# Pinning the small work of an attention + squared-ReLU kernel to fixed places between the tile products

## The chip, the cores and the metric

One core of a Trainium2 chip runs the whole program. The metric is device time in microseconds (us). The engines named below are TensorE (PE, with its weight loads PEld), VectorE (DVE), ScalarE (ACT), GpSimd (POOL) and SyncE (SP), which here only issues transfers. Each engine works through its own list of instructions in order; semaphores make one wait for another.

## The reference

For each of 4 batches (12,480 rows of 128 numbers, 49 agents) agents attend to keys and values, queries attend to agents, and the product goes through a wide layer with a squared ReLU:

```python
def sm(a, b):
    s = scale * (a @ b.transpose(0, 2, 1))
    e = np.exp(s - s.max(-1, keepdims=True))
    return e / (e.sum(-1, keepdims=True) + 1e-09)
agent_v = sm(agents, k) @ v              # 49 x 128 per batch
x = sm(q, agents) @ agent_v              # 49,920 x 128 in all
h = np.maximum(x @ w_in, 0.0)            # 128 -> 2048
out = (h * h) @ w_out                    # 2048 -> 128
```

## The kernel before

The rows are cut into 52 groups of 960 (13 in each batch), a group into two halves of 480 columns. Because `sm(q, agents) @ agent_v @ w_in` is one small table times the query weights, the hidden layer is made from a per-batch table (`aw_hi`, `aw_ex`, 2048 columns, made by `tables`) and per-group query weights (`w`, `x`, made by `queries`). Numbers that must be exact are split into a rounded half and a rest (`hi`, `lo`; `g_hi`, `g_lo`), which TensorE multiplies one after the other.

The unit of the main loop is a *session*: two steps k and k+1, 416 sessions in all, 8 to a group and 104 to a batch. In a session TensorE does four products `h<-w,aw_hi` and four narrow ones `h<-x,aw_ex` (19 rows each, side by side) in `first`, and twelve products `o<-...` of the steps four back in `second`. For each of the two steps (`hidden`) ScalarE makes the ReLU `r<-h` and the square `g_hi<-r`, VectorE multiplies `r*h`, and the rest `g_lo` comes from GpSimd (step k, whose product stands in the tile `gg`: two instructions of 480) or from VectorE (step k+1, whose product `h<-r,h` stays in PSUM). The hidden tiles `h` are three pairs of PSUM banks, and a session uses two of them. So the second pair of products of a session is written over the tile of step k of the session before, and has to wait until VectorE has made `gg` from it.

Beside that runs small work for what comes next. For the next batch, `background`: 13 times `scores` (keys), `maxima`, 13 times `values`, `tables`. A value block is `d<-s,mb` on GpSimd, the exponential of `d` on ScalarE, a rounding cast on ScalarE and a difference on GpSimd for the weights `e` and for the values `vs`, and eight products into the one spare PSUM bank `psa`. For the next group, `queries`: eight products, a maximum and a subtraction on VectorE, an exponential on ScalarE, a sum, an addition and a reciprocal (`z`) on VectorE, a scaling on GpSimd (`e<-e,z`), cast and difference (`pp`), eight products with the identity `identr` that turn the weights over (L312, four to a half), a copy `w<-psa` on ScalarE, and five small copies by transfer for each half.

What sets the order: the main loop's own instructions on PE, ACT and DVE are chained in the order written (`queued`, L337). All small work, GpSimd's rests (L372) and all transfers are placed by the scheduler, which estimates when each becomes ready; `step` only spreads them over the sessions (`SPREAD`). The first batch's table and the first query weights are made ahead of the loop, whose first products start 83.71 us into the span.

Of the kernel before, what the change touches and what calls it, by code (L numbers as in the profile page):

```python
# [17 lines left out]
P = 128  # L18
# [10 lines left out]
QAT = 3  # L29
WIN = 4  # L30
# [4 lines left out]
SPREAD = 0.88  # L35
# [3 lines left out]
def agent_attention_relu2(ctx: ExitStack, tc: tile.TileContext, qT, kT, v, agT, w_in, w_out, outT):  # L39
    nc = tc.nc  # L40
    C, NTOK = qT.shape
# [9 lines left out]
    NQ = P // 32  # L51
    scale = 1.0 / math.sqrt(C)

# [6 lines left out]
    dec = ctx.enter_context(tc.tile_pool(name="dec", bufs=2))  # L60
    ps_h = ctx.enter_context(tc.tile_pool(name="ps_h", bufs=3, space=PSUM))
# [9 lines left out]
    identr = const.tile([TP, TP], F32R, name="identr")  # L71
    nc.scalar.copy(identr, ident[:TP, :TP])
# [54 lines left out]

    alone = [True]

    def bank():  # L130
        if alone[0]:
            return ps_h.tile([P, 2, 512], F32, name="h")[:, 0, :]
        return ps_a.tile([P, 512], F32, name="psa")


# [3 lines left out]
    def load_keys(b, i, pool, name):  # L139
        kt = pool.tile([C, BLK], F32, name=name)  # L140
        nc.sync.dma_start(kt, kT[:, b * N + i * BLK : b * N + (i + 1) * BLK])
        return kt

    def load_values(b, i, pool, name):
        vt = pool.tile([TP, NT, C], F32, name=name)
        src = v[b, i * BLK : (i + 1) * BLK, :].rearrange("(p t) c -> p t c", p=TP)
        last[nc.sync] = nc.sync.dma_start(vt, src)
        return vt

    def scores(b, i, kt):  # L150
        st = state.setdefault(b, {"s": []})
        ps = bank()
        sv = ps[:TP, : NT * NA].rearrange("p (t a) -> p t a", a=NA)
        for t in range(NT):
            nc.tensor.matmul(sv[:, t, :], kt[:, t * TP : (t + 1) * TP], ag[:, b, :], start=True, stop=True)  # L155
        yield
        s = sp.tile([TP, NT, NA], F32, name="s")
        nc.scalar.copy(s, sv)
        if i == 0:
            st["mx"] = small.tile([TP, NT, NA], F32, name="mx")  # L160
            nc.vector.tensor_copy(st["mx"], sv)
        else:
            nc.vector.tensor_max(st["mx"], st["mx"], sv)  # L163
        st["s"].append(s)

    def maxima(b):
        st = state[b]
        m1 = small.tile([TP, NA], F32, name="m1")
        nc.vector.reduce_max(m1, st["mx"].rearrange("p t a -> p a t"), axis=AX.X)
        yield  # L170
        pt = bank()
        nc.tensor.transpose(pt[:NA, :TP], m1, ident[:TP, :TP])
        yield
        m2 = small.tile([NA, 1], F32, name="m2")
        nc.vector.reduce_max(m2, pt[:NA, :TP], axis=AX.X)
        dg = small.tile([NA, NA], F32, name="dg")
        nc.vector.tensor_scalar_mul(dg, ident[:NA, :NA], m2)
        yield
        pb = bank()
        nc.tensor.matmul(pb[:TP, :NA], ones[:NA, :TP], dg, start=True, stop=True)  # L180
        yield
        st["mb"] = small.tile([TP, NA], F32, name="mb")
        nc.vector.tensor_copy(st["mb"], pb[:TP, :NA])

    def halves(out, x, n, eng):

        w = x.shape[2]
        nc.scalar.copy(out[:, :, :w], x)  # L188
        yield
        last[eng] = eng.tensor_sub(out[:, :, n : n + w], x, out[:, :, :w].bitcast(F32))  # L190

    def whole_values(b, i, vt):
# [10 lines left out]
        if i == 1:  # L203
            st["es"] = small.tile([TP, NT, NA], F32, name="es")
# [14 lines left out]
    def values(b, i, vt, eng):  # L219
        st = state[b]  # L220
        s = st["s"][i]
        mb = st["mb"].rearrange("p (o a) -> p o a", o=1).broadcast_to([TP, NT, NA])
        d = small.tile([TP, NT, NA], F32, name="d", bufs=2)
        eng.tensor_sub(d, s, mb)
        W = 2 * (C + 1)
        vs = split[i % 2]
        yield from halves(vs, vt, C + 1, nc.gpsimd)
        yield
        nc.scalar.activation(d, d, AF.Exp, scale=scale)
        e = small.tile([TP, NT, K2], F32R, name="e2", bufs=2)  # L230
        yield from halves(e, d, NA, eng)
        yield
        pv = bank()
        for t in range(NT):
            nc.tensor.matmul(pv[:K2, :W], e[:, t, :], vs[:, t, :], start=(t == 0), stop=(t == NT - 1))  # L235
        yield
        if i == 0:
            st["av"] = small.tile([K2, W], F32, name="av")
            nc.vector.tensor_copy(st["av"], pv[:K2, :W])
        else:  # L240
            nc.vector.tensor_add(st["av"], st["av"], pv[:K2, :W])  # L241

    def tables(b):
        st = state[b]
        qd = quad.rearrange("p h a -> p (h a)")
        if "x" not in st:
            st["x"] = small.tile([K2, C + 1], F32, name="x")
            nc.vector.tensor_add(st["x"], st["av"][:, : C + 1], st["av"][:, C + 1 :])
        x = st["x"]
        yield  # L250
        pa = bank()
        nc.tensor.matmul(pa[:C, :K2], x[:, :C], qd, start=True, stop=True)
        nc.tensor.matmul(pa[:K2, K2 : K2 + 1], qd, x[:, C:], start=True, stop=True)
        yield
        av = small.tile([C, K2], F32, name="avT")
        nc.scalar.copy(av, pa[:C, :K2])
        rl = small.tile([K2, 1], F32, name="rl")
        nc.vector.tensor_scalar_add(rl, pa[:K2, K2 : K2 + 1], 1e-9)
        nc.vector.reciprocal(rl, rl)
        hi = st["hi"] = aw.tile([P, FF], F32R, name="aw_hi")  # L260
        ex = st["lo"] = aw.tile([P, NCH // NQ, P], F32R, name="aw_ex")
        for n in range(FF // 512):
            yield
            cs = slice(n * 512, (n + 1) * 512)
            pw = bank()
            nc.tensor.matmul(pw[:K2, :], av, win[:, cs], start=True, stop=True)  # L266
            yield
            last[nc.scalar] = nc.scalar.activation(hi[:K2, cs], pw[:K2, :], AF.Copy, scale=rl)
            lo = aw.tile([NA, 512], F32R, name="aw_lo", bufs=3)
            last[nc.vector] = nc.vector.scalar_tensor_tensor(  # L270
# [3 lines left out]
            yield  # L274
            nc.sync.dma_start(hi[K2:, cs].bitcast(F32), lo[:SP, :].bitcast(F32))
            for t in range(NQ):
                nc.sync.dma_start(ex[t * 32 : t * 32 + NL, n, :].bitcast(F32), lo[SP:, t * P : (t + 1) * P].bitcast(F32))


    weights = {}  # L280

    def queries(g):
        b = g // NB
        qt = qp.tile([C, BLK], F32, name="qt", bufs=1)
        nc.sync.dma_start(qt, qT[:, g * BLK : (g + 1) * BLK])
        yield
        ps = bank()
        sv = ps[:TP, : NT * NA].rearrange("p (t a) -> p t a", a=NA)
        for t in range(NT):
            nc.tensor.matmul(sv[:, t, :], qt[:, t * TP : (t + 1) * TP], ag[:, b, :], start=True, stop=True)  # L290
        yield
        m = qp.tile([TP, NT, 1], F32, name="m", bufs=1)
        nc.vector.reduce_max(m, sv, axis=AX.X)
        e = qp.tile([TP, NT, NA], F32, name="e", bufs=1)
        nc.vector.tensor_sub(e, sv, m.broadcast_to([TP, NT, NA]))
        yield
        nc.scalar.activation(e, e, AF.Exp, scale=scale)
        yield
        z = qp.tile([TP, NT, 1], F32, name="z", bufs=1)
        nc.vector.reduce_sum(z, e, axis=AX.X)  # L300
        nc.vector.tensor_scalar_add(z, z, 1e-9)  # L301
        nc.vector.reciprocal(z, z)
        nc.gpsimd.tensor_mul(e, e, z.broadcast_to([TP, NT, NA]))
        yield
        pp = qp.tile([TP, NT, K2], F32R, name="pp", bufs=1)
        yield from halves(pp, e, NA, nc.gpsimd)
        weights[g] = []
        for j in range(2):
            yield
            pt = bank()  # L310
            for t in range(NT // 2):
                nc.tensor.matmul(  # L312
                    pt[:K2, t * TP : (t + 1) * TP], pp[:, j * (NT // 2) + t, :], identr, start=True, stop=True
                )
# [223 lines left out]
```

## Time and profile before

| | |
|---|---|
| three runs | 2061.34, 2061.95 (median), 2062.36 us |
| profiled execution | 2060.99 us, span 2059.2 us |
| granted TensorE clock, mean | 0.992 |
| busy: PE, ACT, DVE, POOL | 2029.8, 1782.3, 1686.1, 1279.2 us |
| largest POOL group, `g_lo` (L372) | 832 x 1222 ns |
| turning products `psa<-identr,pp` (L312) in the loop | 408 x 243 ns, in 102 places |

Busy time counts an engine as busy while any of its instructions runs. Matmuls overlap, so the time that a TensorE product really takes is read from the starts in the chain of waits or the timeline, not from its length. In the timeline a row has the start, the length, engine, line, operation, tiles written and read, shapes, count, and in brackets the idle time ahead and what ended it. `SPq` is SP's transfer queue, and the length there is what it took to issue the transfer.

### The profile page before, as it was taken

Reading aid. Unit: us, or ns where it says so; the run is one execution under the profiler, and the core shown is the slowest. Engines: PE = TensorE matmul, PEld = TensorE weight load, DVE = VectorE, ACT = ScalarE, POOL = GpSimd, SP = SyncE. Lnnn points to the kernel's source line nnn. Section 1 sums busy time; section 2 is a strip of 40 time slices with the busy share of each in tenths; the row PEclk is TensorE's granted clock in tenths of the full one; section 3 lists DMA queues with packets and bytes.
Section 4 is the critical chain, followed back from the end, with each engine's and each line's share of the span. In section 5 each row is a group of like instructions: output and inputs, shape, how many; then the busy total and the mean of one; then the engine's idle time right before and its main releaser. Section 6 shows DMA issues by size and latency. Waiting matters only on the chain.

```text
span 2059.2 us, 31857 instructions
## 1 busy us (share of the span) xinstructions
PE 2029.8 (99%) x11014; PEld 1589.8 (77%) x11014; DVE 1686.1 (82%) x1842; ACT 1782.3 (87%) x2100; POOL 1279.2 (62%) x1104
## 2 busy tenths in 40 slices
PE   9799999999999999999999999999999999999999
PEld 8588777777788777777778877777777777777777
DVE  5687888888887888888887788888888888888887
ACT  3478999989888899989888899998889898989897
POOL 3555787765544587776555467877555555656555
PEclk9799999999999999999999999999999999999999
DMA  9532122121122221221112212211111111111100
GB/s 288 160 92 76 59 72 74 53 77 41 45 81 65 62 72 54 72 71 57 55 54 69 68 42 61 74 58 49 42 50 36 45 36 46 37 41 36 38 23 20
DMA packets 55604, 131.36 MB, mean 64 GB/s; under 512 B 6660, under 2 KB 34388, under 8 KB 55444
## 3 DMA queue, kind: packets, MB, share of 16 engines
q1 hardware_dynamic: 55444, 129.33, 21.0%
q8 instruction: 88, 1.44, 0.3%
q14 instruction: 72, 0.59, 0.1%
HBM read 80.97 MB, written 25.56 MB: 52 GB/s over the span
## 4 chain that ended last, share of the span: by engine, by line
PE 53%; DVE 1%; issue 0%; ACT 0%
PE o L337 33%; PE h L337 16%; PE psa L290 2%; PE psa L155 1%; PE psa L312 1%; PE psa L235 1%; PE psa L266 0%; DVE h L337 0%; DVE gg L337 0%; DVE g_lo L337 0%; DVE z L301 0%; ACT r L337 0%; DVE ob L337 0%; ACT g_hi L337 0%; DVE av L241 0%
## 5 line engine op out<-in xcount | busy, mean ns | idle before, releaser
L372 POOL TENSOR_TENSOR g_lo<-gg,g_hi 128x480 fp32r<-128x480 f32 x832 | 999.2, 1222 | 685.7 <-DVE gg L337 489.1
L337 ACT ACTIVATE r<-h 128x960 f32<-128x960 f32 x832 | 800.9, 963 | 150.0 <-PE h L337 141.9
L337 ACT ACTIVATE g_hi<-r 128x960 fp32r<-128x960 f32 x832 | 837.7, 1007 | 34.1 <-POOL e L190 0.7
L337 DVE TENSOR_TENSOR h<-r,h 128x960 f32<-128x960 f32 x416 | 482.4, 1160 | 160.2 <-ACT r L337 157.8
L337 DVE TENSOR_TENSOR gg<-r,h 128x960 f32<-128x960 f32 x416 | 477.8, 1149 | 81.9 <-ACT r L337 81.0
L337 PE MATMUL o<-g_hi,wo_hi 128*128 128x480 f32 x1664 | 543.0, 408 | 0.0
L337 DVE TENSOR_TENSOR g_lo<-h,g_hi 128x960 fp32r<-128x960 f32 x416 | 480.8, 1156 | 45.2 <-ACT g_hi L337 8.1
L337 PE MATMUL o<-g_hi,wo_lo 128*128 128x480 f32 x1664 | 498.7, 381 | 0.0
L337 PE MATMUL o<-g_lo,wo_hi 128*128 128x480 f32 x1664 | 497.7, 380 | 0.0
L337 PE MATMUL h<-w,aw_hi 128*128 128x480 f32 x1664 | 483.3, 398 | 9.7 <-DVE gg L337 8.1
L337 PEld LDWEIGHTS o<-g_hi,wo_hi 128*128 128x128 f32 x1664 | 280.8, 188 | 118.8 <-issue 70.1
L337 PEld LDWEIGHTS o<-g_hi,wo_lo 128*128 128x128 f32 x1664 | 313.4, 188 | 51.3
L337 PEld LDWEIGHTS o<-g_lo,wo_hi 128*128 128x128 f32 x1664 | 313.0, 188 | 50.9
L337 PEld LDWEIGHTS h<-w,aw_hi 128*128 128x128 f32 x1664 | 289.0, 190 | 56.9 <-DVE gg L337 17.5
L337 PE MATMUL h<-x,aw_ex 19*128 19x480 f32 x1664 | 205.4, 481 | 0.1
L337 PEld LDWEIGHTS h<-x,aw_ex 19*128 19x128 f32 x1664 | 80.5, 182 | 140.7 <-issue 139.7
L290 PEld LDWEIGHTS psa<-ag,qt 128*120 128x120 f32 x816 | 102.2, 187 | 7.8 <-issue 1.4
L337 DVE COPY ob<-o 128x480 f32<-128x480 f32 x104 | 68.3, 656 | 39.8 <-PE o L337 38.3
L290 PE MATMUL psa<-ag,qt 128*120 128x49 f32 x816 | 98.1, 264 | 0.0
L190 POOL TENSOR_TENSOR vs<-vt,vs 120x1024 fp32r<-120x1024 f32 x39 | 86.3, 2213 | 16.7 <-ACT vs L188 16.4
L155 PEld LDWEIGHTS psa<-ag,kt 128*120 128x120 f32 x624 | 74.7, 185 | 4.8 <-DVE mx L163 0.6
L155 PE MATMUL psa<-ag,kt 128*120 128x49 f32 x624 | 71.9, 262 | 0.2 <-DVE mx L163 0.2
(109 smaller groups left out, 1026.6 us busy)
## 6 DMA issues: line engine op xcount, KB each, us to landing
qt<-in_qT SPq DMA_DIRECT2D x52, 480.0 KB
out_T<-ob SPq DMA_DIRECT2D x104, 240.0 KB
kt<-in_kT SPq DMA_DIRECT2D x39, 480.0 KB
vt<-in_v SPq DMA_DIRECT2D x39, 480.0 KB
x<-w SPq DMA_DIRECT2D x416, 35.6 KB
ahead<-in_kT SPq DMA_DIRECT2D x13, 480.0 KB
ahead<-in_v SPq DMA_DIRECT2D x13, 480.0 KB
w<-w SPq DMA_DIRECT2D x104, 56.2 KB
```

Source lines behind the costliest of these rows:

```text
L155: nc.tensor.matmul(sv[:, t, :], kt[:, t * TP : (t + 1) * TP], ag[:, b, :], start=True, stop=True)
L190: last[eng] = eng.tensor_sub(out[:, :, n : n + w], x, out[:, :, :w].bitcast(F32))
L235: nc.tensor.matmul(pv[:K2, :W], e[:, t, :], vs[:, t, :], start=(t == 0), stop=(t == NT - 1))
L290: nc.tensor.matmul(sv[:, t, :], qt[:, t * TP : (t + 1) * TP], ag[:, b, :], start=True, stop=True)
L312: nc.tensor.matmul(pt[:K2, t * TP : (t + 1) * TP], pp[:, j * (NT // 2) + t, :], identr, start=True, stop=True)
L337: ins = issue(*args, **kw)
L372: nc.gpsimd.tensor_sub(lo[:, n, :], gg[:, n, :], hi[:, n, :].bitcast(F32))
```

## The change

- Every instruction of the loop, small work, GpSimd's rests and SP's transfers included, is chained in the order written (`Pinned`). The scheduler no longer chooses.
- The small work is written as lanes of generators that ask for a place: "B" is a use of the spare bank, between the four main products (`main`) and the four narrow ones (`rest`); "A" and "D" are one piece for ScalarE and VectorE, behind step k's own work and again at the session's end; "G" and "S" are GpSimd's and SP's, at the session's end only. A session has room for one B, two G (a "GG" takes both) and three S.
- GpSimd takes over the roundings of the values, of their weights and of the query weights, which ScalarE did.
- The query weights are no longer turned by products and copied by ScalarE. VectorE turns 32x32 blocks (`et`), GpSimd rounds and takes the rest, two transfers write both to DRAM, eight transfers read them back in the new layout, and five copies fill the rest of `w` and `x` for both halves at once. Queries are 128 instead of 120 to a tile (the host pads them), and a group's chain starts nine sessions ahead.
- In `fill` each lane may move on by one piece; the query lane is asked first.

TensorE, ahead of a half's first session, before: the turning products stand among the main products.

```order
L337 MATMUL o<-g_lo,wo_hi 128x480 x2
L337 MATMUL h<-w_11444,aw_hi 128x480 x2
L312 MATMUL psa<-identr,pp 98x120 x4
L337 MATMUL h<-w_11444,aw_hi 128x480 x2
L337 MATMUL h<-x_11445,aw_ex 128x480 x4
L337 MATMUL o<-g_hi,wo_hi 128x480 x2
```

After, a session with a small piece on TensorE (`qt` are the queries, `ag` the agents):

```order
L64 MATMUL o<-g_lo,wo_hi 128x480 x2
L64 MATMUL h<-w,aw_hi 128x480 x4
L64 MATMUL psa<-ag,qt 128x49 x8
L64 MATMUL h<-x,aw_ex 128x480 x4
L64 MATMUL o<-g_hi,wo_hi 128x480 x2
```

The turning products are gone, and a small piece stands always between the main and the narrow products.

GpSimd at a value block before: `d` is taken ahead of the session's rests `g_lo`.

```order
L372 TENSOR_TENSOR g_lo_2535<-gg_2531,g_hi_2533 128x480 x2
L224 TENSOR_TENSOR d_3357<-s_1325,mb_1979 120x392
L190 TENSOR_TENSOR pp_2619<-e_2562,pp_2619 120x8x49
L372 TENSOR_TENSOR g_lo_2582<-gg_2578,g_hi_2580 128x480 x2
L372 TENSOR_TENSOR g_lo_2637<-gg_2633,g_hi_2635 128x480 x2
```

ScalarE before, at the same block: the exponential stands behind the squares of the session whose rest on GpSimd is `g_lo_2582`.

```order
L337 ACTIVATE g_hi_2580<-r_2576 128x960
L337 ACTIVATE r_2598<-h_2567 128x960
L337 ACTIVATE g_hi_2601<-r_2598 128x960
L229 ACTIVATE d_3357<-d_3357 120x392
L337 ACTIVATE r_2631<-h_2621 128x960
```

GpSimd at a value block after:

```order
L64 CAST vs1_107<-vt_2317 120x8x128
L64 TENSOR_TENSOR g_lo_2679<-gg_2675,g_hi_2677 128x480 x2
L64 TENSOR_TENSOR d_2707<-s_1137,mb_1849 120x392
L64 TENSOR_TENSOR g_lo_2726<-gg_2722,g_hi_2724 128x480 x2
L64 CAST e2_2751<-d_2707 120x8x49
```

ScalarE at that block after:

```order
L64 ACTIVATE g_hi_2677<-r_2673 128x960
L64 ACTIVATE r_2695<-h_2655 128x960
L64 ACTIVATE g_hi_2698<-r_2695 128x960
L64 ACTIVATE d_2707<-d_2707 120x392
L64 ACTIVATE r_2720<-h_2710 128x960
```

`d` now comes behind the session's rests, and its exponential still stands behind that same session's squares and ahead of the next session's first ReLU.

VectorE after, from a query's session on (`m` maximum, `z` sum and reciprocal, `et` the turned weights):

```order
L64 TENSOR_REDUCE m_2824<-psa_2802 128x8
L64 TENSOR_TENSOR qe_96<-psa_2802,m_2824 128x8x49
L64 TENSOR_TENSOR h_2797<-r_2841,h_2797 128x2x480
L64 TENSOR_TENSOR g_lo_2846<-h_2797,g_hi_2844 128x960
L64 TENSOR_REDUCE z_2850<-qe_96 128x8
L64 TENSOR_SCALAR z_2850<-z_2850 128x8
L64 RECIPROCAL z_2850<-z_2850 128x8
L64 TENSOR_TENSOR gg_2875<-r_2873,h_2854 128x960
L64 TENSOR_TENSOR av_2148<-av_2148,psa_2860 98x258
L64 TENSOR_TENSOR h_2855<-r_2895,h_2855 128x2x480
L64 TENSOR_TENSOR g_lo_2900<-h_2855,g_hi_2898 128x960
L64 STREAM_TRANSPOSE et_2906<-qe_96 128x8x2x32
```

The last row is new; it stands one session behind `z`, and waits for GpSimd's scaling of the same session.

The diff, cut to what the text below speaks of:

```diff
+    def queued(issue, eng, *args, **kw):
+        if not steady[0]:
+            return issue(*args, **kw)
+        with tc.issue_after(chain[eng]) if eng in chain else ExitStack():
+            ins = issue(*args, **kw)
+        chain[eng] = ins.ins
+        return ins
+    pe, act, dve, pool, sp_ = (Pinned(e) for e in (nc.tensor, nc.scalar, nc.vector, nc.gpsimd, nc.sync))
...
-        yield from halves(vs, vt, C + 1, nc.gpsimd)
-        yield
-        nc.scalar.activation(d, d, AF.Exp, scale=scale)
+    def value_halves(vt, vs, out):
+        yield "G"
+        pool.tensor_copy(vs[:, :, :C], vt)
+        yield "GG"
+        last[nc.gpsimd] = pool.tensor_sub(vs[:, :, C + 1 : 2 * C + 1], vt, vs[:, :, :C].bitcast(F32))
+    def value_weights(b, i, out):
+        yield "G"
+        d = small.tile([TP, NT, NA], F32, name="d", bufs=2)
+        pool.tensor_sub(d, st["s"][i], mb)
+        yield "A"
+        act.activation(d, d, AF.Exp, scale=scale)
+        yield "GG"
+        pool.tensor_copy(e[:, :, :NA], d)
+        last[nc.gpsimd] = pool.tensor_sub(e[:, :, NA:], d, e[:, :, :NA].bitcast(F32))
...
-        yield from halves(pp, e, NA, nc.gpsimd)
-                nc.tensor.matmul(
-                    pt[:K2, t * TP : (t + 1) * TP], pp[:, j * (NT // 2) + t, :], identr, start=True, stop=True
-                )
-            nc.scalar.copy(w[:K2, :], pt[:K2, :G])
+        yield "G"
+        pool.tensor_mul(e, e, z.broadcast_to([P, NT, NA]))
+        yield "D"
+        dve.transpose(et.rearrange("p a t i -> p t a i"), qe.rearrange("p t (a i) -> p t a i", i=32))
+        yield "GG"
+        pool.tensor_copy(hi, et)
+        last[nc.gpsimd] = pool.tensor_sub(lo, et, hi.bitcast(F32))
+        yield "S"
+        for y in (hi, lo):
+            d = turn.tile([P, 4, HT * TW], F32, name="d")
+            sp_.dma_start(d, y.rearrange("p (x t) i -> p x (t i)", t=HT).bitcast(F32))
+        yield "S"
+        for n, y in enumerate(flat):
+            for j in range(2):
+                sp_.dma_start(to[n * NA : n * NA + 32], y[:, j, :, :])
+                sp_.dma_start(to[n * NA + 32 : (n + 1) * NA], y[: NA - 32, 2 + j, :, :])
+        yield "S"
+        sp_.dma_start(w[K2:, :, :].bitcast(F32), w[:SP, :, :].bitcast(F32))
+        for t in range(NQ):
+            sp_.dma_start(x[t * 32 : t * 32 + NL, :, :].bitcast(F32), w[SP:NA, :, :].bitcast(F32))
...
+            hs, outs = main(k)
+            fill("B", 1)
+            rest(k, outs)
+            r, gg = square(k, hs[0])
+            divide(k, r, gg)
+            fill("A", 1)
+            fill("D", 1)
+        for n in range(2):
+            if k + n >= LAG:
+                second(k + n - LAG)
+        copied_out()
+            r, gg = square(k + 1, hs[1])
+            divide(k + 1, r, gg)
+        write_out()
+        fill("S", 3)
+        fill("G", 2)
+        fill("A", 1)
+        fill("D", 1)
```

More of the change, by code (lines that the diff above doesn't have):

```diff
@@ L330, in agent_attention_relu2, with main @@
     acc = {}
-    chain = {}
-    def queued(issue, eng, *args, **kw):
-        with tc.issue_after(chain[eng]) if eng in chain else ExitStack():
-            ins = issue(*args, **kw)
-        chain[eng] = ins.ins
-        return ins
-    def first(k):
+    def main(k):
         g, i = divmod(k, SLOTS)
@@ new lines, in weights_lane, with sums_lane, after @@
+    def weights_lane(b, out, used):
+        for i in range(NB):
+            while i - len(used) >= 2:
+                yield "-"
+            yield from value_weights(b, i, out)
+    def sums_lane(b, weighted, halved, used):
+        for i in range(NB):
+            while min(len(halved), len(weighted)) <= i or now[0] < max(halved[i][0], weighted[i][0]):
+                yield "-"
+            yield from value_sums(b, i, weighted[i][1], halved[i][1])
+            used.append(i)
+    def after(gens, then):
+        while any(g in lanes for g in gens):
+            yield "-"
+        yield from then()
@@ new lines, in agent_attention_relu2, with start, fill @@
+    lanes = {}
+    def start(gen, ahead=False):
+        later = dict(lanes) if ahead else {}
+        if ahead:
+            lanes.clear()
+        lanes[gen] = next(gen)
+        lanes.update(later)
+        return gen
+    def fill(what, most):
+        for gen in list(lanes):
+            tag = lanes[gen]
+            if tag == "-":
+                tag = lanes[gen] = next(gen, None)
+                if tag is None:
+                    del lanes[gen]
+                    continue
+            if tag == "B":
+                if what != "B" or free[0] is None or now[0] < free[0]:
+                    continue
+            elif tag[0] != what:
+                continue
+            if len(tag) > most:
+                continue
+            most -= len(tag)
+            lanes[gen] = next(gen, None)
+            if lanes[gen] is None:
+                del lanes[gen]
+            if most <= 0:
+                return
@@ L428, in run, with then @@
+    def background(b):
+        keys = start(keys_lane(b))
+        def then():
+            yield from maxima(b)
+            e, v, used = [], [], []
+            ends = [start(gen) for gen in (sums_lane(b, e, v, used), weights_lane(b, e, used), halves_lane(b, v, used))]
+            yield "-"
+            yield from after(ends, lambda: tables(b))
+        start(after([keys], then))
     def run(gen):
@@ L455, in agent_attention_relu2 @@
                 load_w_in(dec, WIN + i)
+        q0 = queries(0)
+        next(q0)
         next(q0)
```

352 lines of the change are left out of this document (187 added, 165 removed).

## The prediction

> **What bounds the kernel now.** I read the page first, then the busy time by stage, then the chain of waits in the last batch, which has no background, then single sessions in the timeline.
>
> ```profile
> PE 2029.8 (99%) x11014; PEld 1589.8 (77%) x11014; DVE 1686.1 (82%) x1842; ACT 1782.3 (87%) x2100; POOL 1279.2 (62%) x1104
> ```
>
> ```profile
> 1100.00:1596.00 496.00, 494.59 (x2673) 385.69 (x2671) 407.93 (x437) 444.04 (x522) 320.89 (x272) 1.00 0.18 55
> 1596.00:2046.00 450.00, 450.00 (x2318) 346.76 (x2318) 384.12 (x391) 409.46 (x456) 265.70 (x229) 1.00 0.11 36
> ```
>
> The rows of stages give length, then busy time of PE, PEld, DVE, ACT and POOL, then the clock. TensorE has 1.4 us of idle time in the third batch and none in the last, at a full clock. So a product taken away is time gained, and any wait put ahead of a product is time lost.
>
> ```profile
> 1685.67 2.82 PE o L337 x12
> 1688.49 0.32 PE psa L312 x4
> 1688.81 1.34 PE h L337 x7
> 1690.15 2.83 PE o L337 x12
> 1692.98 1.30 PE h L337 x8
> 1694.28 2.81 PE o L337 x12
> ...
> 1721.04 2.81 PE o L337 x12
> ```
>
> From one `o` to the next is a session: 1690.15 to 1694.28, bare, is 4.13; 1685.67 to 1690.15, with four turning products, is 4.48. Eight sessions, 1685.67 to 1721.04, take 35.37.
>
> The next rows are a session with nothing in its way.
>
> ```profile
> 1006.76 0.49 PE L337 MATMUL h<-x,aw_ex 19*128 19x480 f32 x4
> 1007.31 0.97 ACT L337 ACTIVATE r<-h 128x960 f32<-128x960 f32 x1 [0.46 <-PE h L337]
> 1008.38 1.15 DVE L337 TENSOR_TENSOR gg<-r,h 128x960 f32<-128x960 f32 x1
> 1009.70 2.41 POOL L372 TENSOR_TENSOR g_lo<-gg,g_hi 128x480 fp32r<-128x480 f32 x2
> 1009.91 1.04 PE L337 MATMUL h<-w,aw_hi 128*128 128x480 f32 x4
> ```
>
> I count from the end of the narrow products, T = 1006.76 + 0.49 = 1007.25. ReLU starts at T+0.06, `gg` ends at T+2.28, GpSimd's rests run T+2.45 to T+4.86, and the next main products start at T+2.66. Their second pair, two steps of 0.22 later (1.04 less one length of about 0.6, over two), needs `gg`: about T+3.1. So ReLU may start some 0.75 late before TensorE feels it. One session shows the stall itself.
>
> ```profile
> 228.49 0.49 PE L337 MATMUL h<-x,aw_ex 19*128 19x480 f32 x4
> ...
> 229.31 2.21 POOL L190 TENSOR_TENSOR vs<-vt,vs 120x1024 fp32r<-120x1024 f32 x1
> ...
> 229.55 0.97 ACT L337 ACTIVATE r<-h 128x960 f32<-128x960 f32 x1
> ...
> 230.25 1.30 DVE L301 TENSOR_SCALAR z<-z 120x8 f32<-120x8 f32 x1
> ...
> 231.65 0.60 PE L337 MATMUL h<-w,aw_hi 128*128 128x480 f32 x2
> 231.70 1.12 DVE L337 TENSOR_TENSOR gg<-r,h 128x960 f32<-128x960 f32 x1
> ...
> 232.87 0.70 PE L337 MATMUL h<-w,aw_hi 128*128 128x480 f32 x2 [0.63 <-DVE gg L337]
> ```
>
> Here T is 228.98; `gg` starts behind `z` at T+2.72 instead of T+1.13, 1.6 late, and the second pair at 232.87 instead of 231.65 + 0.44 = 232.09, 0.8 late: 1.6 less the slack of 0.75. So a session forgives three quarters of a microsecond, and the rest is on the path.
>
> **The change part by part.** The sum is made against the profiled execution, 2060.99 us (span 2059.2 and 1.8 around it), which stands 1.0 below the median.
>
> *Turning products removed.* 102 places in the loop at 4.48 - 4.13 = 0.35 to 0.36: -37. All of it is on the path.
>
> *Queries of 128.* Weight loads are longer by 8/120. A query costs 35.37 - 8 x 4.12 - 0.71 = 1.70; 51 x 1.70 x 8/120 = +6 at most, 0 at least. Weight loads are part of the path here, so I take 6.
>
> *Waits of today.* In the waits view, TensorE's waits for others in the loop:
>
> ```profile
> PE h L337 <- DVE gg L337: 8.1, 9, 3.2
> ...
> PE h L337 <- DVE aw_lo L270: 1.2, 1, 1.2
> ```
>
> The first row comes from where the scheduler put the small work, and goes with it: -8 (0 to -8). The second is the start of the loop, which waits for the first table, not for the first query weights; their new way over DRAM lies beside the value loads there: 0 (-3 to 5).
>
> *ScalarE's casts and copies.*
>
> ```profile
> L317 ACT CAST w<-psa 98x480 fp32r<-98x480 f32 x102 | 55.7, 546 | 2.8 <-PE psa L312 1.6 <-PE h L337 0.3
> ...
> L188 ACT CAST vs<-vt 120x1024 fp32r<-120x1024 f32 x39 | 40.4, 1038 | 0.1
> ...
> L188 ACT CAST pp<-e 120x392 fp32r<-120x392 f32 x52 | 26.7, 513 | 0.0
> ...
> L188 ACT CAST e<-d 120x392 fp32r<-120x392 f32 x39 | 20.0, 520 | 0.0
> ```
>
> 143 us leave ScalarE, which is not the bound: worth 0, since TensorE's own work covers them today.
>
> *The exponential of a value block.*
>
> ```profile
> L224 POOL TENSOR_TENSOR d<-s,mb 120x392 f32<-120x392 f32 x39 | 37.2, 961 | 0.0
> L229 ACT ACTIVATE d<-d 120x392 f32<-120x392 f32 x39 | 19.9, 518 | 0.0
> L303 POOL TENSOR_TENSOR e<-e,z 120x392 f32<-120x392 f32 x52 | 44.0, 846 | 15.9 <-DVE z L302 13.0 <-ACT r L337 3.0
> ...
> L295 DVE TENSOR_TENSOR e<-psa,m 120x392 f32<-120x392 f32 x51 | 28.7, 563 | 1.3
> L337 DVE COPY ob<-o 128x480 f32<-128x480 f32 x104 | 68.3, 656 | 39.8 <-PE o L337 38.3
> ```
>
> No idle time stands before L229 now. In the new order `d` follows GpSimd's rests: T+4.86+0.96 = T+5.82; the exponential ends at T+6.34. Behind it on ScalarE is the next ReLU, which should start at T+4.12+0.06. It is 2.15 late; less 0.75 of slack, 1.4 on the path. Of 13 blocks to a batch, two have a query's products (1.70) in the next session, which cover it. Of the other eleven, the order puts a piece of about 0.85 to 0.96 ahead on GpSimd in six, or its end spills over from the session before: 1.4 + 0.8 = 2.2. In the five others it is 1.4, from which I take 0.1 for the overlap of neighbours on an engine. 5 x 1.3 + 6 x 2.1 = 19 a batch, three batches: +57. The ends: 0, if later sessions have slack that I don't see, and 33 x 2.9 = 96 with a whole value piece (2.21) ahead at every third.
>
> *Turning on VectorE.* It takes 512 elements; nearest row the `ob` copy, 0.66 (480 from PSUM). It waits for GpSimd's scaling: T+4.86+0.85 = T+5.71, done T+6.4, where the next `gg` should start at T+4.12+1.13 and can be late by 0.75: 0.4 over. In the session before, VectorE does two query pieces of 0.56, `z` and its own work at once, which makes `gg`, and with it GpSimd, about half a microsecond later: 0.9. A following small piece on TensorE covers it; by the order 12 queries of the first three batches and 12 of the last have none: 24 x 0.9 = +22 (0 to 40).
>
> *GpSimd's new casts.*
>
> ```profile
> L190 POOL TENSOR_TENSOR e<-d,e 120x392 fp32r<-120x392 f32 x39 | 37.3, 960 | 0.9 <-ACT e L188 0.9
> L235 PE MATMUL psa<-vs,e 120*98 120x258 f32 x312 | 43.8, 283 | 0.0
> ```
>
> No row shows a large cast there; I bound it by a third of and by the whole two-input piece of its size (2.21, 0.96): 0.7 to 2.2 and 0.3 to 1.0. By the order a value block takes four sessions. GpSimd's four sessions have 4 x 2.41 of rests, 2.21 + 0.96 + 0.96, casts of 1.0 to 3.2, and half a query's pieces (0.85, a cast, a rest of 1.2), 1.3 to 1.6: 16.1 to 18.6. TensorE's have 4 x 4.12, 43.8/39 = 1.1 for the sums and 0.85 for half a query: 18.4. Covered by TensorE, so 0; without that cover the rests `g_lo` come late next, and with them the `o` products.
>
> *SP's transfers, pinned.* 15 issues to a query instead of 10:
>
> ```profile
> 1693.70 0.34 SPq L382 DMA_DIRECT2D out_T<-ob  x1
> ...
> 1698.75 0.85 SPq L320 DMA_DIRECT2D w<-w  x1
> 1699.69 2.48 SPq L322 DMA_DIRECT2D x<-w  x4
> ```
>
> ```profile
> SPq L534 <- DMA out_T<-ob: 1.6, 1, 1.6
> ```
>
> In the session after the turn GpSimd ends its rests at T+4.86, 0.9 late as above, and the cast and rest of `et` 2.4 later (twice the 1.2): T+8.2. Then the write, 0.34 + 1.6, eight reads at 0.85 each, 1.6 until they land, 0.85 + 2.48 to issue the copies, and 1.6: T+23.5. The narrow products that need `x` end six bare sessions, a query and 3.7 us later, T+30.1. 6.6 to spare, so 0 (the bound above is in a rival); key, value and output transfers queue behind it on SP, and are wanted two sessions or more after their place.
>
> Sum: -37 + 6 - 8 + 57 + 22 = +40: 2061 + 40 = **2101 us**, 1.9% slower.
>
> **Two pages weighed.** The `z` addition of 8 elements took 1.30 and ended at 231.55; GpSimd's value piece ended at 231.52. The Trainium skill, SBUF — State Buffer (Who interferes with whom), says that a one-input VectorE instruction in a two-port mode and a GpSimd instruction exclude each other for their whole length. The trace agrees, and by it three queries a batch, where GpSimd starts a value piece at that session's end, would pay about 1 more: 2110 instead of 2101.
>
> **The rivals.**
>
> *Waits fall into slack (faster).* At 0.5 or less per exponential instead of 1.3 to 2.1, and no cost of the turn: -39 + 33 x 0 to 0.5 = 2022 to 2039; it decides at 39/33 = 1.2 us per exponential. For it: ScalarE loses 143 us of other work. Against: it takes its list in order, and the stalled session above paid all that went beyond 0.75.
>
> *The two cancel:* waits between 35 and 43 us: 2061, no change.
>
> *`x` comes late (slower still).*
>
> ```profile
> q1 hardware_dynamic: 55444, 129.33, 21.0%
> ```
>
> 129.33 MB in 21.0% of 16 engines' 2059 us is 18.7 KB per us and engine. If the four copies of 19 rows x 3840 B ran one behind another on one engine, they would take 4 x 3.9 = 15.6 instead of 2.48, 13.1 later: 6.5 past the 6.6 to spare, for the 17 or so queries with bare sessions behind them (11 in the last batch, two before the end of each other): 2101 + up to 110 = 2211. It decides at 6.6 us. The Trainium skill, DMA: Bandwidth & Descriptors (Why a DMA increments its semaphore by 16 and not by 1), says that a transfer uses the largest number of engines up to 16 that divides its slowest dimension: one for 19 rows and for 17. No view shows engines per transfer. By the page's 436 GB/s over 16 engines my estimate is 4 x 2.7 and 1 to 2 us late, 2101 + 25.
>
> *GpSimd is the bound in the value stage:* casts at the two-input price, over by 0.2 a block of four sessions, and by about 1 where GpSimd also waits for its inputs: 39 x 0.2 to 1.0, 2109 to 2140. For it: its four sessions come close to TensorE's; against: TensorE's own stalls lengthen the sessions and let it catch up.
>
> **How the numbers follow.** A change of under 0.2% (4 us) can't be told from none. Forecast 0.47; late `x` 0.16; GpSimd bound 0.09; cancelling 0.07; faster 0.21. So slower 0.72, same 0.07, faster 0.21. Within its own bounds (half to one and a half of each wait) the forecast runs from 2062 to 2140. The range takes in half of the faster rival and the small ends of the slower two: 2035 to 2150.
>
> **What would show it.** Right: ScalarE idle before `d<-d`, ended by POOL `d`, some 2 us, 33 times or so; PE idle before `h<-w,aw_hi` put to DVE `gg`, 60 to 90 us in all; bare sessions still 4.12; no `psa<-identr`. Wrong: those idle times near zero, or PE waiting for `x`, `w`, `kt` transfers or for POOL `g_lo`.

## The result, and the profile after

The changed kernel takes 2229.73 us (median; 2224.96 to 2230.67) against 2061.72, a ratio of 1.081 (95% interval 1.079 to 1.083): slower, as forecast, but by 168 us and not by 40. The profiled execution took 2224.96 us, its span is 2223.2.

The page's first part has the busy time of each engine:

```profile
PE 2062.5 (93%) x10598; PEld 1601.7 (72%) x10598; DVE 1712.3 (77%) x1894; ACT 1680.9 (76%) x1865; POOL 1374.1 (62%) x1235
```

The 416 turning products are gone (11,014 less 10,598), and yet TensorE is busy 33 us longer than before, and idle for 161 us instead of 29. So there are two losses: waits, and products that take longer. The granted clock of the stages shows the second; these are three batches with background and the last, with length, busy time of PE, PEld, DVE, ACT and POOL, then the clock:

```profile
112.00:658.00 546.00, 502.30 (x2543) 388.04 (x2542) 408.23 (x439) 404.24 (x446) 346.45 (x309) 0.96 0.25 76
658.00:1203.00 545.00, 508.55 (x2616) 395.32 (x2615) 419.10 (x453) 416.60 (x461) 352.42 (x312) 0.97 0.27 80
1203.00:1747.00 544.00, 509.02 (x2618) 396.35 (x2617) 419.91 (x455) 416.81 (x461) 352.90 (x313) 0.97 0.27 80
1747.00:2210.00 463.00, 449.06 (x2237) 341.43 (x2236) 390.98 (x407) 399.68 (x425) 276.65 (x242) 1.00 0.18 59
```

Before, the third and fourth batch stood at 1.00. The waits view tells of the first (who waits for whom: us in total, times, longest):

```profile
ACT d L64 <- POOL d L64: 96.0, 39, 4.8
...
PE h L64 <- DVE gg L64: 77.4, 85, 4.4
...
DVE et L64 <- POOL qe L64: 38.6, 43, 1.2
...
PE h L64 <- DMA x<-w: 27.6, 13, 3.0
...
DVE aw_lo L64 <- DMA aw_ex<-aw_lo: 23.6, 4, 7.9
PE psa L64 <- DVE aw_lo L64: 21.7, 3, 7.4
```

The first three rows are what the prediction told of: the exponential waits for `d`, the turn for the scaling, and TensorE for `gg` (8.1 before). The last three it had at zero: late copies of `x`, and a table whose copies come late. Each is shown below by one place in the timeline.

*The exponential.* `d` behind the rests, a value block without cover:

```profile
222.81 0.96 POOL L64 TENSOR_TENSOR d<-s,mb 120x392 f32<-120x392 f32 x1
...
223.81 0.53 ACT L64 ACTIVATE d<-d 120x392 f32<-120x392 f32 x1 [2.07 <-POOL d L64]
...
226.51 0.69 PE L64 MATMUL h<-w,aw_hi 128*128 128x480 f32 x2 [1.39 <-DVE gg L64]
```

ScalarE waits 2.07 and TensorE 1.39: worked out were "some 2 us" and 1.4. The session, from 224.52 to 230.29, takes 5.77 instead of 4.12. Where GpSimd's rests themselves start late, the wait is longer. In the session ahead of the next rows VectorE ends `gg` only at 509.45, at the same time as GpSimd ends a piece of a query. Here something else follows (TensorE alone):

```profile
513.28 0.60 PE L64 MATMUL h<-w,aw_hi 128*128 128x480 f32 x2
515.65 0.70 PE L64 MATMUL h<-w,aw_hi 128*128 128x480 f32 x2 [1.78 <-DVE gg L64]
...
517.25 1.00 PE L64 MATMUL o<-g_hi,wo_lo 128*128 128x480 f32 x2
518.05 1.00 PE L64 MATMUL o<-g_lo,wo_hi 128*128 128x480 f32 x2
...
520.45 0.68 PE L64 MATMUL o<-g_lo,wo_hi 128*128 128x480 f32 x2
520.97 1.03 PE L64 MATMUL h<-w,aw_hi 128*128 128x480 f32 x4
```

From 517.25 on two products take 0.80 instead of 0.44, because the clock is halved. All slow stretches of this trace behind 111 us last 3.41 us or three or four times that, and they start on one grid: 517.22, 773.22 and 855.14, for example, are 75 and 24 steps of 3.413 apart. The next rows are steps of this grid; the last columns are clock, share of DMA and GB/s. The last two stand around the wait above, the first three around another wait of 1.78:

```profile
266.61 0.60 PE L64 MATMUL h<-w,aw_hi 128*128 128x480 f32 x2
268.99 0.70 PE L64 MATMUL h<-w,aw_hi 128*128 128x480 f32 x2 [1.78 <-DVE gg L64]
```

```profile
264.63:268.04 3.41, 2.58 (x12) 1.88 (x10) 0.76 (x2) 1.73 (x3) 1.62 (x2) 1.00 0.30 67
268.04:271.45 3.41, 2.46 (x12) 1.72 (x13) 2.60 (x3) 3.38 (x4) 2.35 (x2) 1.00 0.30 70
271.45:274.87 3.42, 3.42 (x18) 2.40 (x17) 3.00 (x4) 3.36 (x5) 3.06 (x5) 1.00 0.09 29
...
513.80:517.22 3.42, 1.64 (x9) 0.98 (x9) 2.10 (x2) 3.36 (x5) 1.45 (x2) 1.00 0.25 57
517.22:520.63 3.41, 3.41 (x10) 2.82 (x9) 3.00 (x4) 3.35 (x5) 3.04 (x4) 0.50 0.14 39
```

At 515.65 the whole wait lies in one step, and the next step runs at half clock. At 268.99 it lies on two, with 0.83 and 0.95 of idle time, and the clock stays. With the slow step the session took 7.69 instead of 4.12; without it, from 266.61 to 272.77, 6.16. Of the twelve waits for `gg` of 1.7 us or more behind 111 us, nine were met by a slow step and three were not (at 268.99, 392.21 and 1326.81). The 1.39 above had none.

*The copies of `x`*, first query of the loop:

```profile
138.84 2.46 SPq L64 DMA_DIRECT2D x<-w  x4
...
146.15 0.76 PE L64 MATMUL h<-x,aw_ex 19*128 19x480 f32 x1
...
149.53 0.76 PE L64 MATMUL h<-x,aw_ex 19*128 19x480 f32 x1 [2.62 <-DMA x<-w]
...
152.30 0.76 PE L64 MATMUL h<-x,aw_ex 19*128 19x480 f32 x1 [2.01 <-DMA x<-w]
...
155.14 0.76 PE L64 MATMUL h<-x,aw_ex 19*128 19x480 f32 x1 [2.07 <-DMA x<-w]
```

The four narrow products each read one copy, and the last three are released 3.4, 2.8 and 2.8 us apart: the copies run one behind another. Between two of the releases the share of DMA is that of one engine of sixteen, 0.06:

```profile
149.50:152.20 2.70, 0.76 (x1) 0.28 (x1) 0.80 (x1) 1.84 (x2) 0.00 (x0) 0.50 0.06 24
```

*A table*, at the end of a batch:

```profile
560.86 2.47 SPq L64 DMA_DIRECT2D x<-w  x4
...
564.63 4.67 SPq L64 DMA_DIRECT2D aw_ex<-aw_lo  x4
...
577.63 0.74 DVE L64 SCALAR_TENSOR_TENSOR aw_lo<-psa,rl,aw_hi 49x512 fp32r<-49x512 f32 x1 [7.72 <-DMA aw_ex<-aw_lo]
...
578.43 3.65 PE L64 MATMUL psa<-ag,qt 128*128 128x49 f32 x16 [7.23 <-DVE aw_lo L64]
```

The last quarter's low half waits for a free buffer, whose copies were issued right behind the query's copies of `x` and land 13 us later. The next query's products want the bank that this quarter holds, and all of TensorE stands behind them. The diff had cut `aw_lo` from three buffers to two. At the start of the loop the first product waits for such a copy too (6.9 us for `aw_hi<-aw_lo` in the waits view), and the loop starts at 88.1 instead of 83.7.

*The turn*, last batch:

```profile
1826.94 0.86 POOL L64 TENSOR_TENSOR qe<-qe,z 128x392 f32<-128x392 f32 x1
...
1827.84 0.71 DVE L64 STREAM_TRANSPOSE et<-qe 128x512 f32<-128x512 f32 x1 [1.06 <-POOL qe L64]
...
1829.64 0.70 PE L64 MATMUL h<-w,aw_hi 128*128 128x480 f32 x2 [0.78 <-DVE gg L64]
```

### The profile page after: what moved, and what is told of

It is laid out like the page before. It is cut to its first block, busy times and chain, and to the rows that moved or that the text cites. A ratio compares the mean times of both kernels' runs of the same rounds, so it can differ in the third digit from the quotient of the medians.

```text
span 2223.2 us, 30964 instructions
## 1 busy us (share of the span) xinstructions
PE 2062.5 (93%) x10598; PEld 1601.7 (72%) x10598; DVE 1712.3 (77%) x1894; ACT 1680.9 (76%) x1865; POOL 1374.1 (62%) x1235
## 5 line engine op out<-in xcount | busy, mean ns | idle before, releaser
L64 PE MATMUL o<-g_hi,wo_hi 128*128 128x480 f32 x1664 | 553.2, 414 | 0.0
L64 PE MATMUL h<-w,aw_hi 128*128 128x480 f32 x1664 | 462.9, 391 | 88.6 <-DVE gg L64 77.4
L64 PE MATMUL o<-g_hi,wo_lo 128*128 128x480 f32 x1664 | 510.4, 388 | 0.0
L64 PE MATMUL o<-g_lo,wo_hi 128*128 128x480 f32 x1664 | 508.2, 387 | 0.0
L64 PEld LDWEIGHTS h<-w,aw_hi 128*128 128x128 f32 x1664 | 304.0, 189 | 181.0 <-DVE gg L64 124.6
L64 PEld LDWEIGHTS o<-g_lo,wo_hi 128*128 128x128 f32 x1664 | 321.0, 193 | 53.1
L64 PE MATMUL h<-x,aw_ex 19*128 19x480 f32 x1664 | 215.4, 488 | 27.6 <-DMA x<-w 27.6
L64 PEld LDWEIGHTS psa<-ag,qt 128*128 128x128 f32 x816 | 107.0, 205 | 26.0 <-DVE aw_lo L64 22.9
L64 PE MATMUL psa<-ag,qt 128*128 128x49 f32 x816 | 104.4, 285 | 21.7 <-DVE aw_lo L64 21.7
L64 ACT ACTIVATE d<-d 120x392 f32<-120x392 f32 x39 | 20.7, 532 | 96.0 <-POOL d L64 96.0
```

Source lines behind the costliest of these rows:

```text
L64: ins = issue(*args, **kw)
```

## The experiments

Each kernel is the changed one with the edit shown; the sums and what is built on them say so. All are set against the kernel before, on the same chip.

**Four buffers for `aw_lo`**

```diff
-            lo = aw.tile([NA, 512], F32R, name="aw_lo")
+            if n < 2:
+                lo = aw.tile([NA, 512], F32R, name="aw_lo")
+            else:
+                lo = small.tile([TP, NT, K2], F32R, name="e2", bufs=2).rearrange("p t a -> p (t a)")[:NA, :512]
```

> Only edit to the changed kernel: the four pieces of a table's low half (aw_lo) get four buffers instead of two (the third and fourth use the value weights' two buffers, idle then), so that VectorE need not wait for the copies of the first two. Theory A (the table's copies through SP's one ordered queue hold VectorE, and it holds the bank and TensorE; sessions 87, 191 and 295 are 10.5 to 11.7 us too long, of which 7.2 is waiting and the rest TensorE at half clock behind it): 3 x 11 = 33 us less, 2197 us, and no wait of DVE aw_lo for DMA aw_ex. Theory B (the queue itself is what is late, and the query's copies, which stand behind the table's, come late instead): 2220 or more, with the wait at x<-w one group later.

2193.38 us, ratio 1.064 (1.0617 to 1.0664): 36 less, as theory A had it. The kernel before had three buffers, which were not run here. VectorE no longer waits for the table's copies in the loop. That does not say why these copies are late; the next run does.

**Copies of 20 rows into `x`**

```diff
-            sp_.dma_start(x[t * 32 : t * 32 + NL, :, :].bitcast(F32), w[SP:NA, :, :].bitcast(F32))
+            sp_.dma_start(x[t * 32 : t * 32 + 20, :, :].bitcast(F32), w[SP : SP + 20, :, :].bitcast(F32))
```

> Only edit to the changed kernel: each of the four copies that fill x moves 20 rows instead of 19 (the twentieth is not read). More bytes, same issues. Theory A (a copy of 19 rows goes over one DMA engine, so the four come 2.8 us apart, as in the first query, and the last is too late in 11 groups; 20 rows spread over ten engines): the four land within 2 us, waits for x<-w go from 27.6 us to under 5, and with the half clock behind them some 40 us are gained: about 2190 us. Theory B (x is late because key, value and query loads of 480 to 512 KB fill all engines in front of it; rows do not matter): 2225 or more, and the narrow products still wait.

2167.25 us, ratio 1.0516 (1.0499 to 1.0534): 62 less, for one row more. At the same query the copies are now issued at 131.14 and all four products run at once, 4 us after the last issue:

```profile
131.14 3.05 SPq L64 DMA_DIRECT2D x<-w  x4
...
138.05 0.49 PE L64 MATMUL h<-x,aw_ex 19*128 19x480 f32 x4
```

In the last batch the four copies of one query are issued from 1855.59 to 1858.62, and SP issues nothing else between 1854.1 and 1859.5; the share of DMA is now

```profile
1857.00:1859.00 2.00, 2.00 (x11) 1.73 (x10) 1.50 (x3) 1.89 (x4) 0.47 (x1) 1.00 0.36 108
```

No wait of TensorE for `x<-w` is left. The gain is larger than the 40 foreseen: the wait of TensorE for `aw_lo` went too (21.7 to 0.7), and the loop starts 9 us earlier (table below). So theory A of the first run named the right wait, but its cause was the same slow copies, which filled SP's queue.

**Copies of 23 rows**

```diff
-            sp_.dma_start(x[t * 32 : t * 32 + NL, :, :].bitcast(F32), w[SP:NA, :, :].bitcast(F32))
+            sp_.dma_start(x[t * 32 : t * 32 + 23, :, :].bitcast(F32), w[SP : SP + 23, :, :].bitcast(F32))
```

> Only edit to the changed kernel: the copies into x move 23 rows instead of 19. Theory A (the number of engines is the largest one up to 16 that divides the rows, so one for 19 and for 23, and ten for 20): each copy takes 23/19 of 2.8 us, the last lands 2.4 us later than with 19, the waits for x<-w grow from 27.6 us to 60 or more and with the half clock behind them the time to 2250 to 2350. Theory B (20 rows were quicker for another reason, such as a count of more than 19 rows): as with 20 rows, about 2167.

2338.06 us, ratio 1.1342 (1.1327 to 1.1358), with

```profile
L64 PE MATMUL h<-x,aw_ex 19*128 19x480 f32 x1664 | 232.7, 493 | 91.0 <-DMA x<-w 91.0
```

So it is not "20 rows or more": 19 and 23 are slow, 20 and (below) 32 quick. The Trainium skill, DMA: Bandwidth & Descriptors (Why a DMA increments its semaphore by 16 and not by 1), has what the rows divide by decide: a transfer uses the largest number of engines up to 16 that divides the slowest dimension. The runs agree with it, and so does the share of 0.06 with 19 rows. But both slow counts are odd and both quick ones even, and an odd count with a larger divisor, such as 21, was not run.

**The exponential one place later**

```diff
         pool.tensor_sub(d, st["s"][i], mb)
+        yield "-"
+        yield "-"
         yield "A"
```

> Only edit to the changed kernel: the exponential of a value block stands one place later on ScalarE, behind step k's ReLU and square of the next session, when GpSimd's d has long been made; all else keeps its place. Theory A (ScalarE's wait for d at the session's end holds the next ReLU, gg and TensorE; the stretched sessions of the value blocks are 24 to 27 us a batch too long): 60 to 76 us less, 2154 to 2170 us, ACT idle before d<-d near 0 instead of 96. Theory B (GpSimd is what is late in the value stage, and its rests g_lo hold the o products as soon as the exponential does not): under 25 us less, above 2205, with waits of PE o for POOL g_lo in the place of those for gg.

2182.4 us, ratio 1.0586 (1.0569 to 1.0603): 47 less, between the two expectations. ScalarE's wait for `d` falls from 96.0 to 8.2, but part of the gain was taken by the next wait in line: TensorE's waits for `x<-w` grew from 27.6 to

```profile
L64 PE MATMUL h<-x,aw_ex 19*128 19x480 f32 x1664 | 220.9, 486 | 41.3 <-DMA x<-w 41.3
```

The copies land no earlier, so behind shorter sessions TensorE waits longer for them.

**`d` ahead of the rests**

```diff
+            fill("P", 1)
             r, gg = square(k, hs[0])
             divide(k, r, gg)
...
-        yield "G"
+        yield "P"
         d = small.tile([TP, NT, NA], F32, name="d", bufs=2)
         pool.tensor_sub(d, st["s"][i], mb)
+        yield "-"
+        yield "-"
         yield "A"
```

> Only edit to the changed kernel: GpSimd takes a value block's d ahead of the session's rests g_lo (as in the kernel before), the exponential keeps its place at the session's end on ScalarE. Theory A (the wait is made by the place of d behind g_lo): ACT idle before d<-d falls from 96 to under 10, and the time by about what moving the exponential gave, 47 us, to 2180; not more, because the late x shows more when the sessions around it are shorter. Theory B (the gain of the moved exponential came from ScalarE's place, not from GpSimd; d ahead makes g_lo a microsecond late instead): 2210 or more, with waits for POOL g_lo.

2156.04 us, ratio 1.0459 (1.0431 to 1.0487): 74 less, 27 more than the moved exponential, though ScalarE's idle time falls as far:

```profile
L64 ACT ACTIVATE d<-d 120x392 f32<-120x392 f32 x39 | 20.1, 516 | 6.5 <-POOL d L64 6.3
```

`d` also leaves one of GpSimd's places at the session's end, so the value lanes get on faster and the value loads stand elsewhere among the copies. With the moved exponential TensorE still waits for the table in three places (21.9 us), here in one (7.1). In the profiled executions the second and third batch, where that wait is gone, are shorter by 7.6 and 14.4 than with the moved exponential, and the other two by 3.7 and 0.3. So most of the 27 us seems to go with the table, and not with the exponential; no run separates them.

**The turn one place later**

```diff
-AHEAD = 1
+AHEAD = 2
...
         pool.tensor_mul(e, e, z.broadcast_to([P, NT, NA]))
+        yield "-"
+        yield "-"
+        yield "-"
         yield "D"
         et = qp.tile([P, 2, NT, 32], F32, name="et", bufs=1)
```

> Only edits to the changed kernel: VectorE turns the query weights one place later (behind step k's product of the next session), and a query's chain starts one session earlier, so that all behind the turn keeps its place. Theory A (the turn's wait for GpSimd's scaling, with the session before it, costs 1.65 to 2.0 in each session pair without cover, 12 in the last batch and about 3 in each other): 30 to 37 us less, 2193 to 2200 us, bare groups of the last batch 34.7 instead of 36.3. Theory B (what is late is GpSimd behind the three z pieces on VectorE, wherever the turn stands): only the later of the two sessions recovers, 18 us less, 2212.

2224.48 us, ratio 1.079 (1.0759 to 1.0821): 5 less, which is inside the spread of its runs (2217 to 2231): no gain, and neither theory. In the last batch the turn's cost is gone (from one query's products to the next 35.23 us, after 36.23), and the other batches lost at least as much (4.4, 4.8 and 8.4). There the turn stands in the one place between VectorE's products, and pushes the key maximum `mx` to the session's end:

```profile
717.36 0.55 DVE L64 TENSOR_TENSOR mx<-mx,psa 120x392 f32<-120x392 f32 x1
717.97 1.33 PE L64 MATMUL psa<-ag,kt 128*120 128x49 f32 x10 [2.61 <-DVE mx L64]
```

The bank that `mx` reads comes free late, and the next session's scores stand in TensorE's list ahead of its narrow products: 2.6 of wait and a slow clock behind, where the turn had cost 1. The earlier chains also put value blocks beside value loads that had not landed. One piece was moved, and with pinned places the neighbours moved with it.

**The scaling ahead of the rests**

```diff
+            fill("P", 1)
             r, gg = square(k, hs[0])
             divide(k, r, gg)
...
-        yield "G"
+        yield "P"
         pool.tensor_mul(e, e, z.broadcast_to([P, NT, NA]))
+        yield "-"
+        yield "-"
+        yield "-"
         yield "D"
```

> Only edit to the changed kernel: GpSimd scales a query's weights (e<-e,z) ahead of the session's rests instead of behind them; the turn on VectorE keeps its place, and no other piece moves. Theory A (the moved turn of the run before lost its gain because a small piece between VectorE's own products pushes av and mx to the session's end, so that the bank comes free late; with the turn left where it is, the wait for the scaling is gone and nothing is pushed): 25 to 36 us less, 2194 to 2205, and bare groups of the last batch at 35 or less instead of 36.3. Theory B (VectorE's own length is what costs, 0.71 behind three pieces of z, not the wait): under 12 us less, 2218 or more.

2168.59 us, ratio 1.0521 (1.0505 to 1.0537): 61 less, twice what theory A gave. The turn waits for nothing:

```profile
L64 DVE STREAM_TRANSPOSE et<-qe 128x512 f32<-128x512 f32 x51 | 35.8, 702 | 0.0
```

and a group of the last batch takes 35.20. That "no other piece moves" was wrong: the scaling, too, leaves a place at the session's end, the tables come eight sessions earlier, and the waits for `x<-w` fall to 10.2. In the last batch, where little else waits, the edit is worth 12.9 us; how much of the rest of the 61 is the turn was not taken apart.

**The three edits together** (32 rows, and `d` and the scaling ahead of the rests), then **with four buffers for `aw_lo`** as well

> Edits to the changed kernel: copies into x of 32 rows instead of 19, and GpSimd takes d and the scaling ahead of the rests. Theory A (three causes, x over one engine, d and scaling behind g_lo; the tables' copies were held by x in the same queue): from the 2167 of the 20-row copies, less 31 us a batch of exponentials and 36 of turns: 2030 to 2050, faster than the kernel before by 0.5 to 1.5%. Theory B (GpSimd is the next bound in the value stage, its pieces and rests together over TensorE's time): 2070 or more, with TensorE waiting for POOL g_lo.

> As the run before, and four buffers for aw_lo. Theory A (the tables wait only while x clogs SP's queue): within 5 us of the run before. Theory B (two buffers are too few by themselves): 10 to 30 us below it, three tables at 3 to 10 each.

2057.73 us, ratio 0.9984 (0.9972 to 0.9996), and 2051.63, ratio 0.9953 (0.9939 to 0.9968). Singly the three edits took 62, 74 and 61 (the first with 20 rows; 32 rows were not run alone); together 172, where the change had cost 168. The first is above theory A's 2030 to 2050 and below theory B's 2070, because what I had counted as the change's own gain is smaller than thought (below). GpSimd is not the next bound: TensorE waits for the values' halves 3.5 us in all with four buffers, and for no rests. The buffers are worth 6 us once `x` is quick, against 36 before, which lies between the two theories and near the first.

The first page row of the last of them answers to the one of after, with as many products:

```profile
PE 1999.1 (98%) x10598; PEld 1573.7 (77%) x10598; DVE 1707.1 (83%) x1894; ACT 1682.1 (82%) x1865; POOL 1376.0 (67%) x1235
```

Its span is 2050.0, so the 173.2 between the two spans are 63.4 in which the same number of products takes longer (2062.5 less 1999.1) and 109.8 of idle time. In the stretches at half clock from 83 us on TensorE is busy for 107.2 us in the changed kernel and for 22.9 here. Half of the difference, some 42 us, is an estimate of what the clock has in the 63.4; the rest was not taken apart. In the last batch one stall a group is left, behind the three pieces of `z`:

```profile
1695.56 0.55 DVE L64 TENSOR_REDUCE z<-qe 128x8 f32<-128x392 f32 x1
1696.15 0.17 DVE L64 TENSOR_SCALAR z<-z 128x8 f32<-128x8 f32 x1
1696.36 0.20 DVE L64 RECIPROCAL z<-z 128x8 f32<-128x8 f32 x1
1696.48 1.11 DVE L64 TENSOR_TENSOR gg<-r,h 128x960 f32<-128x960 f32 x1
...
1697.64 0.70 PE L64 MATMUL h<-w,aw_hi 128*128 128x480 f32 x2 [0.34 <-DVE gg L64]
```

**`z` in two places**, on top of that sum

```diff
         dve.reduce_sum(z, e, axis=AX.X)
+        yield "D"
         dve.tensor_scalar_add(z, z, 1e-9)
...
-            fill("P", 1)
             r, gg = square(k, hs[0])
-            divide(k, r, gg)
+            hi, lo = divide(k, r, gg, False)
             fill("A", 1)
-            fill("D", 1)
+            fill("D", 2)
+            fill("P", 1)
+            for n in range(2):
+                pool.tensor_sub(lo[:, n, :], gg[:, n, :], hi[:, n, :].bitcast(F32))
```

> On top of the sum of the edits (2051.6): of the three pieces of z only the sum stays ahead of the next gg, the addition and the reciprocal go behind it (two pieces may stand there), and GpSimd's place ahead of the rests comes behind them. Theory A (in the last batch a group takes 35.20 where eight bare sessions and a query are 34.6, because the three pieces, 0.92, hold gg by more than the slack; one piece of 0.55 does not): 0.6 less in most of 51 groups, 2022 to 2035. Theory B (the longer list of VectorE is what costs, wherever the pieces stand, or GpSimd's scaling now holds its rests): 2048 or more.

2046.2 us, ratio 0.9925 (0.9912 to 0.9937): 5 less, near theory B. A group goes from 35.20 to 34.99, not to 34.6: the sum alone still holds `gg`, and two sessions are 0.2 too long instead of one 0.6. It is the fastest of all, 0.75% under the kernel before, which is clear of noise but small.

**Value halves from the start of a batch**, on top of that

```diff
-        keys = start(keys_lane(b))
+        e, v, used = [], [], []
+        keys = start(keys_lane(b))
+        halves = start(halves_lane(b, v, used))
```

> As the run before, and the lane of the value halves starts with the keys instead of behind the maxima, so that its first two loads are long landed. Theory A (the first value block's halves wait for their load once, in the first batch, and cost 6.8 us with the half clock behind): 5 to 8 us below the run before. Theory B (the earlier casts and loads only push scores and key loads): no gain, or slower.

2064.67 us, ratio 1.0014 (1.0005 to 1.0023): 18 more, theory B. The wait that it was for is gone, but key loads now land beside value loads and come late:

```profile
637.89 2.08 PE L64 MATMUL psa<-ag,kt 128*120 128x49 f32 x16 [1.41 <-DMA kt<-in_kT]
```

TensorE also waits 2.0 us for `x` of the table on VectorE in each of three batches (5.9 in all), which it did not in the run before, and the loop starts 6.5 us later; why, was not looked into.

Where the edits gain, by the starts of the main products in the timelines of the profiled executions. The first column has the us until the loop's first product, the others the length of each batch:

| kernel | start | 1 | 2 | 3 | 4 |
|---|---|---|---|---|---|
| before | 83.7 | 515.2 | 501.8 | 495.5 | 463.1 |
| after | 88.1 | 569.8 | 545.2 | 543.8 | 476.2 |
| 20 rows | 79.0 | 548.8 | 531.4 | 528.1 | 475.1 |
| `d` ahead | 89.8 | 549.1 | 521.1 | 514.6 | 477.4 |
| scaling ahead | 90.3 | 553.0 | 531.7 | 527.9 | 463.3 |
| sum, four buffers | 80.8 | 513.5 | 496.1 | 496.6 | 463.0 |
| `z` in two places | 78.6 | 519.2 | 493.9 | 494.5 | 460.4 |

## Why the prediction was right and wrong

*The sum.* It had +40, and +168 was measured. Quick copies of `x` alone give 62 back, where the sum had 0. `d` and the scaling ahead of the rests, on top of quick copies, give another 110 (2167 to 2058), where it had 57 + 22 = 79. What is left is 4 us faster than the kernel before, where it had 39 (-37 + 6 - 8). So the 128 us that it missed are 62, 31 and 35. The parts act on each other, and in another order they would divide otherwise.

*Direction and two mechanisms: right.* The exponential and the turn wait for GpSimd pieces put behind the rests, as worked out; both edits that take this away gain, and TensorE's waits for `gg`, 77.4, are inside the 60 to 90 named as a sign. What such a wait costs where it is short was near: 1.65 (5.77 less 4.12) for 1.4, and in the last batch 1.03 a group for 0.9. The sign of being wrong, TensorE waiting for `x`, is there as well.

*SP's transfers, 0: wrong.* This is the step that failed, the largest part of the miss and the one with a cause that the prediction's sum did not have. The 2.48 that I used for the four copies is the time to issue them, not to move them: they take 2.8 each, one behind another. The rival had this mechanism, at 3.9 each, and was given 0.16. By its reckoning 4 x 2.8 = 11.2 is 8.7 more than 2.48, 2.1 past the 6.6 to spare, in every query with bare sessions behind it. That isn't what happened, though the mean of the 13 waits, 27.6 us in all, is 2.1 as well. Three of them are in the first query, and in the last batch, whose sessions are bare, only three queries were late, by 1.48, 0.87 and 0.36; so the 6.6 was too small for most of them, and the equal mean is luck. The sentence on the page's figure has 2.7 a copy, against 2.8 measured; its 25 us were too few, because neither the tables nor the clock were in it.

*The tables: missing.* The cut of `aw_lo` from three buffers to two was in the diff, and the prediction has no term for it. With slow copies of `x` ahead in one ordered queue, four buffers instead of two gain 36 us, in three places; once `x` is quick, 6. Most of these 36 should be part of the 62, since the wait is gone there too.

*The exponential, +57: near in size, with one step wrong.* The waits for `gg` that go with the moved exponential are 49 us (77.4 less 28.5). The two runs gave 47 and 74, the first with 14 more of waits for `x`, the second with two waits for the table fewer. The step that failed here is "less 0.75 of slack, 1.4 on the path": it prices a wait at its own length. At 1.78 the session took 2.0 longer, and 3.6 where the clock was halved behind it. The prediction quoted the clock, 1.00, and kept it.

*The turn, +22:* right in the last batch (13 for 11); the 61 of the whole edit hold other gains, named above.

*The start of the loop, 0:* 4.4 later, inside the bounds of -3 to 5.

*The turning products, -37, and today's waits, -8: right as counts, not as a gain.* The products are gone, but a group without the turn's wait takes 35.20, and before 35.37. Eight bare sessions and a query would be 34.6, so 0.6 of the 0.71 is lost again, and the rows above put it to the three pieces of `z`, which now always stand ahead of `gg`. Splitting them gave back 0.21; the rest, put to the sum, was not taken away by any run. The prediction saw them make `gg` "about half a microsecond later" and forgave it.

*Query weights of 128, +6: wrong, but inside its bounds of 0 to 6.* A weight load of these products went from 184 to 192 ns in the last batch. But the sixteen products took 1.36 + 0.52 there before (rows of twelve and four), and take as much now:

```profile
1814.47 1.88 PE L64 MATMUL psa<-ag,qt 128*128 128x49 f32 x16
```

*ScalarE's casts, 0, and GpSimd's new casts, 0: right.* GpSimd did not become the bound. In the row of after, a large cast takes 1051 ns, inside the bounds.

```profile
L64 POOL CAST vs<-vt 120x1024 fp32r<-120x1024 f32 x39 | 41.0, 1051 | 4.8 <-DMA vt<-in_v 4.8
...
L64 DVE TENSOR_SCALAR z<-z 128x8 f32<-128x8 f32 x51 | 14.2, 278 | 1.7
```

*The rule on VectorE and GpSimd* (the Trainium skill, SBUF — State Buffer, Who interferes with whom): 51 additions at 0.17 would be 8.7, so 5.5 us are spent in long ones, where the prediction's sentence had 9 on the path. The trace does not contradict the rule, and it is a small term.

## What to carry to other kernels

Price a wait of the engine that bounds by what its clock does behind it, not by its length alone: here one of 1.78 us cost 2.0 where the clock stayed, and 3.6 where the next step of its grid was slow. Take the time of a transfer from when its data is used, never from its issue, and look at what its row count divides by. And when places are fixed by hand, a piece that needs another engine belongs behind something that engine has long done; move one piece, and read again what its neighbours now wait for.

## What the runs showed of the hardware

- The clock of TensorE changed only on a grid of 3.41 us. A wait of 1.78 us inside one step was followed by a step at half clock; another of 1.78, and one of 2.54 ahead of the product at 1044.17, lay on two steps and were not. The Trainium skill, TensorE: Matmul & The Clock Gate (Part 1: The HAM clock gate), has the clock go down after an idle window of about 3.4 us. The length of the slow stretch agrees; here less idle time was enough, and the measurement decides.
- One row more made a copy quicker: with 19 rows the four copies came 2.8 us apart, with 0.06 of the DMA engines busy, and cost 62 us; 20 rows left no wait, and 23 rows cost 108 us more than 19.
